# The last group of a Fourier turn gathered in two halves, and the last two dense blocks loaded after the last store

## The chip, the cores and the metric

The kernel runs on one core of one Trainium2 chip. The metric is the device time of one execution in microseconds (us). A profile of one execution is at hand: what each engine did and when, what it waited for, and what the DMA engines moved. TensorE (PE) multiplies matrices, VectorE (DVE) and ScalarE (ACT) work elementwise, GpSimd (POOL) too and more slowly; SyncE (SP) only issues DMAs, and ACT and GpSimd issue some as well. Each of these three has a DMA queue of its own: q1 is SP's, q10 is ACT's, q0 is GpSimd's.

## What is computed

```python
x = A_u                                             # 2048 positions x 512 channels
g = _sigmoid((x * gate_w).sum(-1, keepdims=True))   # one gate per position
a = _A_ref(x, ...)                                  # a long convolution (S4), by FFT, plus a skip term
b = _B_ref(B_x, ...)                                # dense 512 -> 1792, gelu, 1792 -> 512
return g * a + (1 - g) * b
...
K = jnp.einsum("dn,dnl,dn->dl", Cc, P, dB).real     # in _A_ref: a filter of 2048 taps per channel
Yf = Uf * Kf[None, :, :, :]                         # transforms of padded signal and filter, multiplied
y = irfft2(Yf, ...)[:, :, 0, :L]                    # back to positions
```

All of it is in float32; the dense products are made of three matmuls of split operands each (high and low parts).

## The kernel before

The kernel has two parts. `front` computes the dense layers, the filter taps and the first half of the transforms; a planner orders its instructions. `conv`, where the change lies, runs in the order in which it is written, and takes the last 120 us.

**What `conv` does.** A transform of 2048 positions is split into 32 outer by 64 inner steps. `conv` goes through 16 steps s, each with two of the 32 outer frequencies, n = 2s and 2s + 1. For each it transforms signal and taps (`signal`, `taps`, on TensorE), multiplies them (`product`, on VectorE) and transforms back over the inner index (`inverse`). The result of one n is a tile `pa` of 128 partitions by 512 channels. To sum over n, the data must be turned, so that n stands on partitions. `turn` does that through HBM: ScalarE copies `pa` to one of six buffers `sa`, a store of 256 KB writes it to the scratch `t4_d`, and when eight n (one group g of `GROUP` = 8) are stored, gathers bring rows of that group back into `t3`, whose partitions g, g + 4, g + 8, ... they fill. `seat` says on which partition of `t3` a frequency lies, and `constants` lays the rows of the matrix `g1` out to match.

**The queues.** Groups 0 to 2 are stored by SP and gathered by GpSimd, four gathers of 32 partitions by 8 rows of 512 (512 KB) each. Of group 3 the last store, n = 31, is on ACT's queue, and its gathers are eight of 256 KB, in turn on ACT's and SP's queues, since each of them has to wait for the stores to land. Between the stores, at steps 6 to 13, SP also loads eight "dense blocks" with `dense(k)`: the block k of the output that `front` has already written, (1 - g) b, for two tiles of 128 positions (512 KB).

**The end.** While the gathers are under way, TensorE makes late dense products (`rest`): for two position tiles, 2 and 3, seven products of the second dense layer each were put aside by `front`, one takes three matmuls. One of the fourteen runs before the last `inverse`, thirteen after it. A warm-up matmul (`N_KEEP` = 1, into `warm`) follows, and VectorE adds the two late sums to their dense block. Then comes the last turn, m = 0 to 7, called turn groups below: eight matmuls of 64 partitions by 32 columns, which sum over n and give two tiles of 128 positions (`pb`); each needs four of the 32 rows of `t3`. A tile is multiplied by its gate and added to the dense block, on VectorE in one operation, or, for the five tiles in `ASIDE`, by ScalarE and then GpSimd. SP stores each pair (512 KB) to the output, the pairs 0 and 7 tile by tile, the very last tile's on SP and the one before it by the list `(nc.sync, nc.scalar)`.

What sets the order here is the program text alone: each engine and each queue works through its own instructions in order, and waits where an operand is not there.

## Time and profile before

| | |
|---|---|
| median of 3 runs | 516.74 us (516.55 to 516.86) |
| profiled execution | 515.96 us |
| its span, first to last instruction | 514.2 us |
| TensorE busy | 497.0 us (97%) |
| VectorE, ScalarE, GpSimd busy | 427.7, 353.2, 38.7 us |
| DMA | 101.26 MB, 197 GB/s on average |
| granted clock of TensorE over the span | 0.992 |

Busy shares are averages over stages with different limits. TensorE's 97% says that the span is a chain of its work for most of the time, and nothing of the last 30 us, where the question is which transfer or engine comes last. Times below are counted from the span's start.

### The profile page before, as it was taken

To read this page: it belongs to the slowest core of one execution; us is meant where nothing else is said; L and a number is where in the kernel's file an instruction comes from. 1 tells how busy PE (TensorE), PEld (TensorE's weight loads), DVE (VectorE), ACT (ScalarE), POOL (GpSimd) and SP (SyncE) were. 2 spreads that over 40 slices of the span, in tenths; PEclk is the share of its full clock that TensorE was granted. 3 is DMA by queue.
4 is the path that set the end of the run, shared out by engine and by line. 5 is a ranking of instruction groups with operands and counts; after the bars stand their busy time and mean duration, and the time that the engine had idled before them with its cause. 6 is when DMAs were issued, how large, how long until landed. Compare 5 with 4: busy or idle time off the path is not lost.

```text
span 514.2 us, 11207 instructions
## 1 busy us (share of the span) xinstructions
PE 497.0 (97%) x4426; PEld 351.8 (68%) x4426; DVE 427.7 (83%) x794; ACT 353.2 (69%) x545; POOL 38.7 (8%) x74
## 2 busy tenths in 40 slices
PE   8998999989999999999999999999999999999992
PEld 5876787877777878788788888788787533333460
DVE  5989999989999999999999999999711675675533
ACT  6897959499995999977389958686354555555311
POOL 1000000000000000002300310002000001010113
PEclk9998999999999999999999999999999999999998
DMA  8989725172175727433950531716628999999977
GB/s 285 329 287 350 262 88 207 61 222 78 46 243 203 184 88 231 134 101 90 270 114 3 165 42 22 167 23 143 160 56 222 302 329 330 383 396 353 339 281 288
DMA packets 86805, 101.26 MB, mean 197 GB/s; under 512 B 38609, under 2 KB 58129, under 8 KB 86113
## 3 DMA queue, kind: packets, MB, share of 16 engines
q1 hardware_dynamic: 81216, 84.52, 49.8%
q0 software_dynamic: 5056, 14.45, 12.0%
q10 hardware_dynamic: 480, 1.57, 0.8%
q8 instruction: 35, 0.57, 0.5%
q14 instruction: 18, 0.14, 0.1%
HBM read 59.11 MB, written 41.42 MB: 196 GB/s over the span
## 4 chain that ended last, share of the span: by engine, by line
PE 64%; DVE 14%; issue 7%; ACT 7%; DMA 5%; SPq 1%; POOL 1%; POOLq 0%; DVEq 0%; ACTq 0%
PE pz L710 9%; PE ph L900 7%; PE ph L901 7%; PE ph L902 7%; PE acc L946 6%; PE acc L948 6%; PE acc L947 6%; PE p2k L1119 6%; PE p2u L1119 5%; PE pa L1158 5%; PE pz L426 2%; DVE y L675 2%; DVE y L688 2%; DVE loft L521 2%; DVE loft L520 1%
## 5 line engine op out<-in xcount | busy, mean ns | idle before, releaser
L900 PE MATMUL ph<-xh,wh 128*128 128x512 f32 x224 | 89.7, 400 | 1.7 <-ACT io L919 1.7
L901 PE MATMUL ph<-xlo,wh 128*128 128x512 f32 x224 | 88.2, 394 | 0.5 <-DVE xlo L827 0.4
L902 PE MATMUL ph<-xh,wl 128*128 128x512 f32 x224 | 88.0, 393 | 0.0
L946 PE MATMUL acc<-wh,hh 128*128 128x512 f32 x210 | 84.1, 400 | 0.7 <-ACT acc L952 0.7
L948 PE MATMUL acc<-wh,hl 128*128 128x512 f32 x210 | 82.1, 391 | 0.0
L947 PE MATMUL acc<-wl,hh 128*128 128x512 f32 x210 | 81.9, 390 | 0.0
L919 ACT ACTIVATE io<-ph,b1t 128x512 f32<-128x512 f32 x56 | 38.6, 690 | 34.8 <-PE ph L902 29.4
L710 PE MATMUL pz<-y,xc 128*32 128x64 f32 x2048 | 61.6, 290 | 0.4 <-DVE phase L620 0.4
L710 PEld LDWEIGHTS pz<-y,xc 128*32 128x32 f32 x2048 | 57.2, 136 | 6.7 <-issue 3.3
L928 DVE TENSOR_TENSOR hl<-io,hh 128x512 fp32r<-128x512 f32 x56 | 38.5, 687 | 22.7 <-ACT hh L920 22.5
L900 PEld LDWEIGHTS ph<-xh,wh 128*128 128x128 f32 x224 | 42.4, 189 | 14.3 <-ACT io L919 3.4
L901 PEld LDWEIGHTS ph<-xlo,wh 128*128 128x128 f32 x224 | 42.5, 190 | 10.4 <-DVE xlo L827 1.7
L946 PEld LDWEIGHTS acc<-wh,hh 128*128 128x128 f32 x210 | 39.4, 188 | 13.6 <-issue 3.8
L902 PEld LDWEIGHTS ph<-xh,wl 128*128 128x128 f32 x224 | 42.3, 189 | 9.2 <-DVE wl L827 0.3
L675 DVE TENSOR_TENSOR y<-y,ea 128x64 f32<-128x64 f32 (+4 forms) x80 | 45.3, 566 | 0.7 <-POOL y L665 0.4
L948 PEld LDWEIGHTS acc<-wh,hl 128*128 128x128 f32 x210 | 39.4, 188 | 9.0 <-DVE hl L928 0.5
L947 PEld LDWEIGHTS acc<-wl,hh 128*128 128x128 f32 x210 | 39.5, 188 | 7.7
L960 ACT ACTIVATE io<-acc,gate 128x512 f32<-128x512 f32 x30 | 20.3, 686 | 28.9 <-PE acc L948 28.9
L520 DVE TENSOR_TENSOR loft<-xc,zz 128x256 f32<-128x256 f32 (+2 forms) x48 | 37.3, 776 | 0.4
L521 DVE TENSOR_TENSOR loft<-xc,zz 128x256 f32<-128x256 f32 (+2 forms) x48 | 37.2, 774 | 0.0
L1141 DVE TENSOR_TENSOR v<-p2u,k 128x512 f32<-128x512 f32 x16 | 11.1, 691 | 31.1 <-ACT sa L1164 25.3
L688 DVE TENSOR_TENSOR y<-y,loft 128x2048 f32<-128x2048 f32 x16 | 36.6, 2285 | 0.2
(139 smaller groups left out, 840.1 us busy)
## 6 DMA issues: line engine op xcount, KB each, us to landing
tu_d<-attic SPq DMA_DIRECT2D x16, 512.0 KB, 3.5
tk_d<-sk SPq DMA_DIRECT2D x16, 512.0 KB, 6.8
tk<-tk_d SPq DMA_DIRECT2D x32, 256.0 KB, 5.9
t_d<-sa SPq DMA_DIRECT2D x31, 256.0 KB, 5.2
t<-t_d POOLq DMA_DIRECT2D x12, 512.0 KB, 6.9
attic<-tu_d SPq DMA_DIRECT2D x22, 256.0 KB, 4.7
attic<-in_xt_dram SPq DMA_DIRECT2D x20, 256.0 KB, 4.1
attic<-in_xs_dram SPq DMA_DIRECT2D x16, 256.0 KB, 5.3
```

What stands on the lines that cost most here:

```text
L520: vec(2 * m, lambda: vv.tensor_mul(t, a, br), due, [ka, *kb], [kt])
L521: vec(2 * m, lambda: vv.tensor_mul(v, a, bi), due, [ka, *kb], [kv])
L675: nc.vector.tensor_mul(both(n, 64 - 3 * n, n), both(0, 64 - n, n), an)
L688: v.tensor_mul(y[:, 0].rearrange("p (a b) c -> p a b c", a=2), e.rearrange("p (a b) c -> p a b c", a=2), cc,)
L710: nc.tensor.matmul(pk[32 * j : 32 * j + 32, gg // 4, gg % 4], x[:, r, :, ch], y[:, r, :, ch], start=(r == 0), stop=(r == 1), skip_group_ch ...
L900: nc.tensor.matmul(phs[q], h, xh[d], start=(d == 0), stop=False)
L901: nc.tensor.matmul(phs[q], h, xlo[d], start=False, stop=False)
L902: nc.tensor.matmul(phs[q], lo, xh[d], start=False, stop=(d == 3))
L946: nc.tensor.matmul(a, h, wh[1][f], start=(f == 0 and u >= NSB), stop=False, skip_group_check=True)
L947: nc.tensor.matmul(a, h, wl[1][f], start=False, stop=False, skip_group_check=True)
L948: nc.tensor.matmul(a, l, wh[1][f], start=False, stop=(f == FH - 1), skip_group_check=True)
L1119: nc.tensor.matmul(out[64 * i : 64 * i + 64], w, x, start=True, stop=True)
```

## The change

The last group is split by frequency: n = 24 to 27 and n = 28 to 31. The first half goes to a scratch `te_d` whose rows have 16 floats of padding, is gathered by GpSimd as soon as its four stores have landed, in four transfers of 8 partitions by 16 rows, and lies on partitions 3, 7, ..., 31 and 99, 103, ..., 127 of `t3` (the two ends). The second half goes to `tl_d` and lies on partitions 35, 39, ..., 95 (around the middle); all its stores are SP's, and its four gathers (16 partitions by 8 rows, 256 KB) are on ACT's and SP's queues. `seat` and `g1` follow. `dense(6)` and `dense(7)` leave steps 12 and 13 and stand behind the last store. Ten late products are made before the last turn instead of all, and the warm-up matmul is gone. The turn groups go 0, 2, 3, 4, 5, 6, 7, 1; the products left and the addition of the late sums come after the last of them, with the stores of pair 1, tile by tile. `ASIDE` names other tiles.

```diff
@@ constants
-N_KEEP = 1
+N_FIRST = 10
-ASIDE = (2, 4, 7, 9, 12)
+LATE = NT * (BLOCK[-1] + 1) - N_LATE
+ASIDE = (5, 6, 9, 11, 14)
@@ seat
-    return 4 * (n % 8) + n // 8
+    g, k = divmod(n, 8)
+    if g < 3:
+        return 64 * i + 32 * c + 4 * k + g
+    return 64 * i + 32 * (k // 4 ^ i) + 16 * c + 4 * (k % 4) + g
@@ scratch
-    t4_d = dr.tile([4, 2, 2, GROUP, 32, D], F32, name="t4_d")
+    t4_d = dr.tile([3, 2, 2, GROUP, 32, D], F32, name="t4_d")
+    te_d = dr.tile([2, 2, 4, 32, D + 16], F32, name="te_d")
+    tl_d = dr.tile([2, 2, 4, 32, D], F32, name="tl_d")
@@ turn
-                on = nc.sync if n < 31 else nc.scalar
-                on.dma_start(t4_d[g, :, :, k].rearrange("i c q d -> q (i c) d"), sa)
-                if k < GROUP - 1:
-                    continue
-                rows = t4_d[g].rearrange("i c k q d -> (i c k) q d")
-                w = 8 if n < 31 else 4
-                for h in range(0, 32, w):
-                    on = nc.gpsimd if n < 31 else (nc.scalar, nc.sync)[h // w % 2]
-                    on.dma_start(t3[g:P:4, h : h + w], rows[:, h : h + w])
+                to = t4_d[g, :, :, k] if g < 3 else (te_d, tl_d)[k // 4][:, :, k % 4, :, :D]
+                nc.sync.dma_start(to.rearrange("i c q d -> q (i c) d"), sa)
+                if g < 3 and k == GROUP - 1:
+                    rows = t4_d[g].rearrange("i c k q d -> (i c k) q d")
+                    for h in range(0, 32, 8):
+                        nc.gpsimd.dma_start(t3[g:P:4, h : h + 8], rows[:, h : h + 8])
+                if n == 27:
+                    for i in range(2):
+                        rows = te_d[i, :, :, :, :D].rearrange("c k q d -> (c k) q d")
+                        for h in range(0, 32, 16):
+                            nc.gpsimd.dma_start(t3[96 * i + 3 : 96 * i + 32 : 4, h : h + 16], rows[:, h : h + 16])
+                if n == 31:
+                    dense(6)
+                    dense(7)
+                    rows = tl_d.rearrange("i c k q d -> (i c k) q d")
+                    for h in range(0, 32, 8):
+                        on = (nc.scalar, nc.sync)[h // 8 % 2]
+                        on.dma_start(t3[35:96:4, h : h + 8], rows[:, h : h + 8])
@@ the end
-            if 6 <= s < 14:
+            if 6 <= s < 12:
                 dense(s - 6)
-        rest(14)
-        warm = ps.tile([P, D], F32, tag="pa", name="warm", bufs=2)
-        for _ in range(N_KEEP):
-            nc.tensor.matmul(warm[0:64], mats[7][0][1][:, 3], zs[0], start=True, stop=True)
-        for s in range(N_LATE):
-            n = NT - N_LATE + s
-            z = mos[n // 2][:, n % 2]
-            nc.vector.scalar_tensor_tensor(z, accs[n], gate[:, 1, n : n + 1], z, ALU.mult, ALU.add)
-        for m in range(8):
+        rest(N_FIRST)
+        order = [m for m in range(8) if m != LATE // 2] + [LATE // 2]
+        for k, m in enumerate(order):
...
+            if k == 7:
+                rest(14)
...
-                if m in (0, 7):
-                    (nc.sync, nc.scalar)[i if m else 0].dma_start(ov[m, :, i], z)
-            if 0 < m < 7:
+                if k == 0:
+                    nc.sync.dma_start(ov[m, :, i], z)
+            if 0 < k < 7:
                 nc.sync.dma_start(ov[m], mos[m])
+        for i in range(N_LATE):
+            z, g = mos[LATE // 2][:, i], gate[:, 1, LATE + i : LATE + i + 1]
+            nc.vector.scalar_tensor_tensor(z, accs[NT - N_LATE + i], g, z, ALU.mult, ALU.add)
+            (nc.sync, nc.scalar)[i].dma_start(ov[LATE // 2, :, i], z)
```

The names in the rows below: `sa0` to `sa5` are the buffers of the stores, `t4_d`, `te_d` and `tl_d` the scratches, `t3` the gathered data, `attic` and `loft` hold dense blocks, `out_0_dram` is the output; a number at a name's end is a buffer's running number, and `x4` is four in a row. SP's queue before, from the store of n = 22 to the first stores of the output:

```order
L1167 DMA t4_d_61<-sa0_4052 32x4x512
L1167 DMA t4_d_61<-sa1_4053 32x4x512
L1186 DMA attic_76<-out_0_dram 128x1024
L1167 DMA t4_d_61<-sa2_4054 32x4x512
L1167 DMA t4_d_61<-sa3_4055 32x4x512
L1186 DMA attic_76<-out_0_dram 128x1024
L1167 DMA t4_d_61<-sa4_4056 32x4x512
L1167 DMA t4_d_61<-sa5_4057 32x4x512
L1167 DMA t4_d_61<-sa0_4052 32x4x512
L1176 DMA t3_4066<-t4_d_61 32x2048 x4
L1260 DMA out_0_dram<-loft_77 128x512 x2
```

SP's queue in the changed kernel, from the store of n = 24 on:

```order
L1173 DMA te_d_62<-sa0_4054 32x4x512
L1173 DMA te_d_62<-sa1_4055 32x4x512
L1173 DMA te_d_62<-sa2_4056 32x4x512
L1173 DMA te_d_62<-sa3_4057 32x4x512
L1173 DMA tl_d_63<-sa4_4058 32x4x512
L1173 DMA tl_d_63<-sa5_4059 32x4x512
L1173 DMA tl_d_63<-sa0_4054 32x4x512
L1173 DMA tl_d_63<-sa1_4055 32x4x512
L1199 DMA attic_78<-out_0_dram 128x1024 x2
L1189 DMA t3_4068<-tl_d_63 16x4096 x2
L1268 DMA out_0_dram<-loft_79 128x512 x2
```

Two dense blocks that stood before the stores of n = 26 and n = 28 now stand between the last store, which has come over from ACT, and the gathers, of which SP has two instead of four.

TensorE before, from the last late product (three matmuls into `acc3`) to the first turn group (`pb00` and `pb01`):

```order
L1199 MATMUL acc3_4798<-wh15_125,hl5_153 128x512
L1197 MATMUL acc3_4798<-wh16_126,hh6_147 128x512
L1198 MATMUL acc3_4798<-wl16_140,hh6_147 128x512
L1199 MATMUL acc3_4798<-wh16_126,hl6_154 128x512
L1235 MATMUL warm_4820<-z0_4058,f17_4664 64x512
L1247 MATMUL pb00_4824<-t3_4066,g1t_4067 32x512
L1247 MATMUL pb01_4825<-t3_4066,g1t_4067 32x512
L1247 MATMUL pb00_4824<-t3_4066,g1t_4067 32x512
```

In the changed kernel, the same seam:

```order
L1210 MATMUL acc3_4800<-wh13_125,hh3_146 128x512
L1211 MATMUL acc3_4800<-wl13_139,hh3_146 128x512
L1212 MATMUL acc3_4800<-wh13_125,hl3_153 128x512
L1253 MATMUL pb00_4813<-t3_4068,g1t_4069 32x512
L1253 MATMUL pb01_4814<-t3_4068,g1t_4069 32x512
L1253 MATMUL pb00_4813<-t3_4068,g1t_4069 32x512
```

The seam lies three products earlier (`wh13` with `hh3`, not `wh16` with `hh6`), and the warm-up matmul is gone from it. And the end of TensorE's work in the changed kernel, from its last turn group (`pb10`, `pb11`) on:

```order
L1253 MATMUL pb10_4910<-t3_4068,g1t_4069 32x512
L1253 MATMUL pb11_4911<-t3_4068,g1t_4069 32x512
L1210 MATMUL acc3_4800<-wh14_126,hh4_147 128x512
L1211 MATMUL acc3_4800<-wl14_140,hh4_147 128x512
L1212 MATMUL acc3_4800<-wh14_126,hl4_154 128x512
L1210 MATMUL acc3_4800<-wh15_127,hh5_148 128x512
L1211 MATMUL acc3_4800<-wl15_141,hh5_148 128x512
L1212 MATMUL acc3_4800<-wh15_127,hl5_155 128x512
L1210 MATMUL acc3_4800<-wh16_128,hh6_149 128x512
L1211 MATMUL acc3_4800<-wl16_142,hh6_149 128x512
L1212 MATMUL acc3_4800<-wh16_128,hl6_156 128x512
```

The three products that left the seam stand here, behind the last turn group; before, a turn group came last.

## Rows read from the trace of the kernel before

**Rows 1.** Busy time by stage: PE, PEld, DVE, ACT, POOL; clock, DMA share, GB/s.

```profile
478.00:487.00 9.00, 9.00 (x37) 3.44 (x35) 5.16 (x9) 2.98 (x7) 0.62 (x2) 1.00 0.98 348
487.00:497.00 10.00, 10.00 (x42) 7.43 (x41) 1.50 (x2) 0.93 (x2) 0.00 (x0) 1.00 0.79 293
497.00:504.30 7.30, 7.30 (x129) 2.77 (x128) 5.77 (x9) 3.44 (x5) 4.35 (x4) 1.00 0.78 304
```

**Rows 2.** Timeline, the queues of SP and ACT: start, duration in us.

```profile
480.81 1.17 SPq L1167 DMA_DIRECT2D t_d<-sa  x2
...
484.64 3.34 SPq L1167 DMA_DIRECT2D t_d<-sa  x3
...
487.96 0.63 ACTq L1167 DMA_DIRECT2D t_d<-sa  x1
...
491.94 2.57 SPq L1176 DMA_DIRECT2D t<-t_d  x4
...
492.07 2.59 ACTq L1176 DMA_DIRECT2D t<-t_d  x4
...
501.25 1.58 SPq L1262 DMA_DIRECT2D out_dram<-loft  x2
...
506.81 1.12 SPq L1260 DMA_DIRECT2D out_dram<-attic  x1
```

**Rows 3.** DMA issues at 475.3, 480.8, 488.0, 491.9 (two), 506.8: us to landing last.

```profile
t_d<-sa SPq DMA_DIRECT2D x2, 256.0 KB, 2.7
...
t_d<-sa SPq DMA_DIRECT2D x2, 256.0 KB, 6.4
...
t_d<-sa ACTq DMA_DIRECT2D x1, 256.0 KB, 3.8
...
t<-t_d SPq DMA_DIRECT2D x1, 256.0 KB, 3.2
t<-t_d ACTq DMA_DIRECT2D x1, 256.0 KB, 3.7
...
out_dram<-attic SPq DMA_DIRECT2D x1, 256.0 KB, 6.3
```

**Rows 4.** Timeline, the engines from the last store on; brackets tell idle time before.

```profile
487.07 0.50 PE L1197 MATMUL acc<-wh,hh 128*128 128x512 f32 x1
...
495.82 0.39 PE L1199 MATMUL acc<-wh,hl 128*128 128x512 f32 x1
...
496.14 1.07 PE L1235 MATMUL warm<-z,f 128*64 128x512 f32 x2
...
497.14 7.17 PE L1247 MATMUL pb<-t,g1t 64*32 64x512 f32 x128
...
498.32 2.73 DVE L1258 SCALAR_TENSOR_TENSOR loft<-pb,gate,loft 128x512 f32<-128x512 f32 x4 [1.32 <-PE pb L1247]
...
499.95 2.52 POOL L1256 TENSOR_TENSOR loft<-loft,sa 128x512 f32<-128x512 f32 x2 [21.34 <-ACT sa L1255]
...
500.96 5.09 DVE L1258 SCALAR_TENSOR_TENSOR attic<-pb,gate,attic 128x512 f32<-128x512 f32 x7
```

**Rows 5.** DMA queues in 478:484 (two rows), 287:294, 502:511: packets, MB, share.

```profile
q0 software_dynamic: 150, 1.74, 82.8%
q1 hardware_dynamic: 144, 0.53, 22.6%
...
q0 software_dynamic: 979, 1.79, 92.8%
...
DMA  6999999998989999999999999999999999999999
...
DMA packets 1076, 3.55 MB, mean 395 GB/s; under 512 B 110, under 2 KB 110, under 8 KB 1075
```

**Rows 6.** TensorE's timeline at 40.7, and the stretch 41.5:44.9 by engine.

```profile
40.71 1.34 PE L426 MATMUL pz<-attic,c1t 32*64 32x256 f32 x32 [2.07 <-ACT attic L457]
...
41.50:44.90 3.40, 3.40 (x23) 2.35 (x8) 3.40 (x10) 3.40 (x5) 0.00 (x0) 0.50 1.04 383
```

More of the change, by code (lines that the diff above doesn't have):

```diff
@@ L101, in k0_order, with seat @@
     return [8 * (n % 4) + n // 4 for n in range(32)]
-def seat(n):
-    return 4 * (n % 8) + n // 8
+def seat(n, i, c):
+    g, k = divmod(n, 8)
+    if g < 3:
+        return 64 * i + 32 * c + 4 * k + g
+    return 64 * i + 32 * (k // 4 ^ i) + 16 * c + 4 * (k % 4) + g
 def constants():
@@ L124, in constants @@
     c1 = np.concatenate([np.stack([er, ei], 2).reshape(32, 64)] * 4, 0)
-    rows = np.zeros((2, 64, 32))
+    g1 = np.zeros((P, 32))
     for n, k in enumerate(k0_order()):
-        rows[:, seat(n)] = er.T[k] / L
-        rows[:, seat(n) + 32] = ei.T[k] / L
-    g1 = rows.reshape(P, 32)
+        for i in range(2):
+            g1[seat(n, i, 0)] = er.T[k] / L
+            g1[seat(n, i, 1)] = ei.T[k] / L
     ko = k0_order()
@@ L1165, in turn @@
                 g, k = divmod(n, GROUP)
-                on = nc.sync if n < 31 else nc.scalar
-                on.dma_start(t4_d[g, :, :, k].rearrange("i c q d -> q (i c) d"), sa)
-                if k < GROUP - 1:
-                    continue
-                rows = t4_d[g].rearrange("i c k q d -> (i c k) q d")
-                w = 8 if n < 31 else 4
-                for h in range(0, 32, w):
-                    on = nc.gpsimd if n < 31 else (nc.scalar, nc.sync)[h // w % 2]
-                    on.dma_start(t3[g:P:4, h : h + w], rows[:, h : h + w])
+                to = t4_d[g, :, :, k] if g < 3 else (te_d, tl_d)[k // 4][:, :, k % 4, :, :D]
[5 more added lines that the diff above has]
+                if n == 27:
+                    for i in range(2):
+                        rows = te_d[i, :, :, :, :D].rearrange("c k q d -> (c k) q d")
[8 more added lines that the diff above has]
+                        on.dma_start(t3[35:96:4, h : h + 8], rows[:, h : h + 8])
         accs, mos = {}, {}
@@ L1228, in conv @@
             turn(s)
[L1229 removed]
+            if 6 <= s < 12:
                 dense(s - 6)
[L1231 to L1242 removed]
+        rest(N_FIRST)
+        order = [m for m in range(8) if m != LATE // 2] + [LATE // 2]
+        for k, m in enumerate(order):
+            tag, n = ("pa", 2) if k % 3 == 2 else ("pu", 4)
             pbs = [ps.tile([P, D], F32, tag=tag, name=f"pb{m}{i}", bufs=n) for i in range(2)]
```

1 line of the change is left out of this document (removed).

## The prediction, made before the changed kernel had run

> **What bounds the kernel now.** I read the end first, because the diff touches only the last 40 us. By stage, TensorE is busy nearly all of 478 to 504, but what it does from 487 on is filling: thirteen late dense products from 487.07 to 496.2 and a warm-up matmul to 497.2 [rows 1, 4]. What it waits for stands in the queues. The last store of the turn, n = 31, is issued on ACT's queue at 487.96 and lands 3.8 us later, at 491.7 [rows 2, 3]. Only then may the eight gathers of the last group go, four on SP (491.94) and four on ACT (492.07), 2.1 MB in all; their first two land after 3.2 and 3.7 us, at 495.2 and 495.8 [rows 2, 3]. The DMA share of that stage is the lowest of the three (0.78 and 0.79 against 0.98) [rows 1]. The last turn ("turn groups" below: eight groups of eight matmuls, 0.9 us each) starts at 497.14 and takes 7.17 us [rows 4]. So at its start the data was there 1.3 us earlier, and TensorE's filling came last.
>
> After it the order is: VectorE from 498.32 to 506.05 nearly without a gap, GpSimd 1.26 us for each tile put aside, and the stores [rows 4]. The second turn group's store leaves SP at 501.25 [rows 2]; from 502 to 511 the DMA engines move 3.55 MB at 395 GB/s without a slack slice [rows 5]. The last store is issued at 506.81 and lands 6.3 us later, at 513.1 [rows 2, 3]. A store that is queued for 6.3 us instead of 2.7 has some 3.6 us of others ahead of it. So the end is: start of the second turn group (497.14 + 0.9 = 498.0), 3.2 us to its store, then 3.7 MB at the DMA's rate, then a fixed close. A microsecond off the second group's start is a microsecond off the end; one off VectorE's last operation is nothing while that backlog lasts.
>
> **The change, part by part.** *Half of the last group goes early.* Frequencies 24 to 27 get a scratch of their own (te_d); once those four stores have landed, GpSimd gathers them (1.05 MB). What stays behind store 31 is four gathers, 1.05 MB instead of 2.1. *The last two dense blocks* (1.05 MB) leave their places among the stores and go between store 31 and SP's gathers. Bytes up to store 31 are equal: minus 1.05, plus 1.05.
>
> When does store 31 land? It is now SP's, right behind store 30, whose issue ends at 484.64 + 3.34 = 487.98 [rows 2]; so 488.0, as before. Its time to land is bounded by two rows: 2.7 us for stores that met a short queue, 6.4 us for stores 26 and 27, issued into GpSimd's third gather [rows 3]. The rest of the queue is gone by then: stores 26 and 27 had a dense block of 0.52 MB ahead of them, 1.4 us at the 377 GB/s of that stretch (1.74 + 0.53 MB in 6 us) [rows 5], so they land near 486.4, stores 28 and 29 soon after. But the early gather, issued at 486.5 and moving from about 488 (estimate: its four issues and a start of about 1 us), runs just beside stores 30 and 31. I take 3.5 us, between the bounds and nearer to the lower one because its rows are 2 KB pieces like the stores' and not 16 KB: landing at 491.5.
>
> The rate between two queues shows in the third gather: GpSimd's queue with 16 KB rows moved 1.74 MB while SP's, with work waiting, moved 0.53 [rows 5]. [...]
>
> *The first turn group* then needs ACT's first gather: issued 0.33 us after the landing as before, landed 3.7 us later: 491.5 + 0.3 + 3.7 = 495.5. Three of the four early gathers must be there too: at the 257 GB/s that GpSimd's queue made alone with 2 KB rows [rows 5], 1.05 MB takes 4.1 us from 488, so 492.1, and 493 with the landing; cover 2 us.
>
> *TensorE's filling.* Ten products instead of thirteen before the turn: each is 0.68 us (thirteen in 487.07 to 496.2), so TensorE is free at 493.9, 1.6 us before the data. The warm-up matmul (1.07 us) goes. Both cost nothing and stop being the last thing.
>
> *The second turn group* needs SP's first gather, which stands behind the dense blocks on SP's queue. Alone these take 2.7 us at 395 GB/s from about 490.8, to 493.5; SP's gathers would begin to move near 492.9, so 0.6 us are lost there. By bytes it is tighter: from 488 the early gather, stores 30 and 31, the dense blocks and the first two gathers are 3.1 MB, 8.0 us at 390 GB/s, so 496.1 and about 0.6 us to land: 496.7. That is 0.3 us after the time at which TensorE could take it (495.5 + 0.9). I take 496.7 for the second group, against 498.0: **minus 1.3 us**. Bounds: store 31 after 2.7 us gives 495.9, minus 2.1; after 6.4 us it gives 499.4 or later, plus 1.4.
>
> *The two late tiles go last.* Tile pair 1 is turned at the end, the three products left (2.1 us) follow, and VectorE adds two operations of 0.74 us behind its eleven. VectorE's end moves from 8.9 us after the first group's start (506.05) to 10.4, so 505.9, and TensorE's last product to 495.5 + 0.9 + 0.3 + 7.2 - 0.9 + 2.3 = 505.3, ahead of it. The stores ahead keep the DMA busy until the last two (0.52 MB, 1.3 us) would begin, about 513.1 - 1.3 - 1.3 - 1.0 = 509.5: cover about 3 us, and it would be paid one for one beyond it. The tiles put aside keep their count (five) and nearly their places among the groups; zero. GpSimd has nothing between its four new issues and its first addition, 499.95 in the profile [rows 4].
>
> Sum on the profiled execution: 515.96 - 1.3 = 514.7. The runs' median is 516.74, 0.8 above the profiled one; the difference is put on it: **515.4**.
>
> **The rivals.** (1) *The early gather holds up the last stores*, as the third one did: landing at 488.0 + 5.2 to 6.4, 493.2 to 494.4. Second group 498.2 to 499.4, so 516.9 to 518.1. For it: SP's stores landed late each time GpSimd gathered. Against: 16 KB rows then, 2 KB rows now. 0.16. (2) *The change doesn't do what it says:* the dense blocks fill no hole but push SP's gathers back, a full microsecond beyond my 0.3; the early half is won and given back: 516.4. 0.13. (3) *TensorE's clock.* Without the filler, TensorE is idle for 1.6 us at 493.9, and longer if store 31 is late. [...] 0.07. (4) *Slower: the early gather runs on half the engines.* Its transfers have 8 partitions each, where the ones in the trace have 32. If each uses eight engines, and all four the same eight, it has half of 257 GB/s: three of four take 6.1 us from 488; those engines also carry half of the stores and dense blocks (0.79 MB at 198 GB/s, 4.0 us). It lands near 499, and the first group starts there instead of the second at 498.0: about plus 1.9, 518.6. It decides if the third early gather lands after 497.1. [...] 0.10.
>
> **How the numbers follow.** Forecast 0.54, at 515.4 with its own range 514.3 to 516.2. 0.2% is 1.0 us, about what a measurement of this kernel can tell from no change. Faster: 0.48 of the forecast and 0.05 of rival 2, 0.53. Same: 0.06, 0.08 of rival 2, 0.12 of rival 1, 0.06 of rival 3, 0.02 of rival 4: 0.34. Slower: 0.04, 0.01 and 0.08: 0.13. The range goes from 513.9 (store 31 after 2.7 us, less the runs' scatter of 0.3) to 517.5, which leaves out most of rival 4 and the worst of rival 1.
>
> **What would show it.** Right: store 31 landed by 492, the first turn group at 495 to 496 waiting for a DMA and not for TensorE, the second within 1.2 us of it, VectorE's last operation 4 us or more before the last landing. Wrong: landing of stores 30 and 31 after 493 (rival 1); a gap of over 1.5 us between the first two groups with SP's gather as releaser (2); a granted clock of 0.5 between 495 and 503 (3); a first group that waits for GpSimd's gather (4); or VectorE's end within 3 us of the last landing, the cover that I counted on.

## The result, and the profile after

| | before | changed kernel |
|---|---|---|
| median | 516.80 us (516.55 to 516.86) | 521.34 us (521.02 to 524.98) |
| ratio | | 1.0104, 95% interval 1.0065 to 1.0142 |
| profiled execution | 515.96 us | 524.98 us |

The changed kernel is 4.5 us slower, where 1.3 us less was forecast; 521.3 lies above the forecast's range of 513.9 to 517.5. Its profiled execution is the longest of the four; the same kernel, run once more for a second trace, took 521.64 us. That second trace (e1_again) is read first, since it is near the median; "the first trace" is that of the 525.0 us.

The second trace's timeline from the last two stores on (start and duration in us; the brackets tell idle time and what ended it) answers to [rows 2] and [rows 4]:

```profile
487.23 2.54 POOL L1182 DMA_DIRECT2D t<-te_d  x4 [8.23 <-DMA te_d<-sa]
...
487.71 1.16 SPq L1173 DMA_DIRECT2D tl_d<-sa  x2
...
488.96 1.57 SPq L1199 DMA_DIRECT2D attic<-out_dram  x2
...
493.81 1.39 SPq L1189 DMA_DIRECT2D t<-tl_d  x2
...
493.89 1.36 ACTq L1189 DMA_DIRECT2D t<-tl_d  x2
...
500.72 9.27 PE L1253 MATMUL pb<-t,g1t 64*32 64x512 f32 x128 [6.32 <-DMA t<-tl_d]
```

The first turn group starts at 500.72, after 6.32 us in which TensorE waited for a late gather; before it started at 497.14 and waited for nothing but TensorE's own filling. Store 31 is issued 0.6 us behind store 30's 487.71, so at 488.32. The DMA issues of that stretch, one row per issue, answer to [rows 3] (last number: us to landing). They are store 31 (488.32), the first dense block (488.96), SP's first late gather (493.81) and ACT's (493.89):

```profile
tl_d<-sa SPq DMA_DIRECT2D x1, 256.0 KB, 5.4
...
attic<-out_dram SPq DMA_DIRECT2D x1, 512.0 KB, 8.3
...
t<-tl_d SPq DMA_DIRECT2D x1, 256.0 KB, 6.6
t<-tl_d ACTq DMA_DIRECT2D x1, 256.0 KB, 6.7
```

Store 31 took 5.4 us to land and not 3.8, and a late gather 6.7 us and not 3.7. So the turn waits on the path that was to become shorter: 12.4 us from store 31's issue (5.4 + 0.2 + 6.7 + 0.1) to the first turn group, against 9.2 before. By stage (columns as in [rows 1]; the last row is the stretch of the low clock, read by itself):

```profile
478.00:487.00 9.00, 9.00 (x39) 3.44 (x35) 5.40 (x9) 3.08 (x6) 0.99 (x2) 1.00 0.92 336
487.00:494.40 7.40, 7.40 (x32) 5.55 (x30) 0.00 (x0) 1.07 (x2) 2.48 (x4) 1.00 0.84 243
494.40:500.70 6.30, 0.00 (x1) 0.01 (x1) 0.00 (x0) 0.00 (x0) 0.00 (x0) 0.81 0.92 326
500.70:510.00 9.30, 9.28 (x129) 2.92 (x129) 6.04 (x9) 3.44 (x5) 4.66 (x4) 0.76 0.43 167
...
498.40:505.10 6.70, 4.38 (x48) 1.41 (x56) 2.04 (x3) 0.53 (x1) 0.00 (x0) 0.50 0.36 140
```

Two things stand there. TensorE is idle for all of 494.4 to 500.7, and its granted clock falls in that stage and is still low in the next, at 0.50 from 498.4 to 505.1: the turn groups take 9.27 us instead of 7.17 [rows 4]. The second turn group starts at 502.40, 4.4 us later than before (498.02). And the DMA engines are busy for 0.84 of 487 to 494.4 but move only 243 GB/s, less than the 293 GB/s at a share of 0.79 in [rows 1]: they are not idle, they are slow.

In the first trace the loss is larger, and it lies elsewhere. Store 31, issued at 489.07, landed as soon as forecast, and the late gathers, issued at 491.65 (SP) and 491.74 (ACT), were late by more:

```profile
tl_d<-sa SPq DMA_DIRECT2D x1, 256.0 KB, 2.5
...
t<-tl_d SPq DMA_DIRECT2D x1, 256.0 KB, 10.2
t<-tl_d ACTq DMA_DIRECT2D x1, 256.0 KB, 8.9
```

The turn even started and stopped again, for one of GpSimd's early gathers:

```profile
500.79 1.88 PE L1253 MATMUL pb<-t,g1t 64*32 64x512 f32 x2 [5.62 <-DMA t<-tl_d]
...
504.08 9.04 PE L1253 MATMUL pb<-t,g1t 64*32 64x512 f32 x126 [1.41 <-DMA t<-te_d]
```

From the first turn group to the last landing of the output it is 16.0 us before (497.14 to 513.14) and 17.9 us in the second trace (500.72 to 518.57). Counted from store 31's issue, the last landing comes 5.1 us later than before; 3.2 of them lie ahead of the first turn group and 1.9 behind it.

### The profile page after: what moved, and what is told of

Read it like the earlier page. It is cut to its first block, busy times and chain, and to the rows that moved or that the text cites. A ratio compares the mean times of both kernels' runs of the same rounds, so it can differ in the third digit from the quotient of the medians.

```text
span 523.2 us, 11199 instructions
## 1 busy us (share of the span) xinstructions
PE 499.9 (96%) x4424; PEld 352.0 (67%) x4424; DVE 427.6 (82%) x794; ACT 353.1 (67%) x545; POOL 41.3 (8%) x78
## 4 chain that ended last, share of the span: by engine, by line
PE 61%; DVE 20%; DMA 8%; ACT 6%; issue 2%; SPq 1%; POOL 0%; DVEq 0%; POOLq 0%; ACTq 0%
PE pz L716 8%; PE ph L906 6%; PE ph L907 6%; PE ph L908 6%; PE acc L952 6%; PE p2u L1125 6%; PE p2k L1125 5%; PE acc L954 5%; PE acc L953 5%; PE pa L1164 5%; DMA t<-te_d 3%; DVE loft L527 2%; DVE y L694 2%; PE pz L432 2%; DVE y L681 2%; DVE loft L526 2%
## 5 line engine op out<-in xcount | busy, mean ns | idle before, releaser
L1147 DVE TENSOR_TENSOR v<-p2u,k 128x512 f32<-128x512 f32 x16 | 11.1, 691 | 31.2 <-ACT sa L1170 25.3
```

## The experiments

Executions differ in when store 31 is issued (487.8 to 490.0 in all but one of the traces), which lies ahead of the part in question. So the table counts from that issue: to the start of the first turn group, and to the last landing of the output, both read from each run's own trace. Times are medians, ratios are against the kernel before on the same chip. A trace is of one execution, and not always of one near the median: that of e10 took 526.4 us, that of e16 516.3. Edits are shown against the changed kernel, with parts left out, unless the text names another.

| run | time, us | ratio, 95% interval | to the turn | to the end |
|---|---|---|---|---|
| before | 516.2 to 517.0 | 1 | 9.2 | 25.2 |
| e1_again: changed kernel | 521.64 | 1.0104, 1.0065 to 1.0142 | 12.4 | 30.2 |
| e2_dense_back | 520.00 | 1.0061, 1.0038 to 1.0083 | 10.4 | 27.9 |
| e3_early_on_act | 522.80 | 1.0123, 1.0098 to 1.0149 | 14.7 | 31.1 |
| e4_end_only | 515.85 | 0.9994, 0.9974 to 1.0013 | 8.4 | 24.6 |
| e5_no_pad | 523.35 | 1.0143, 1.0122 to 1.0164 | 13.7 | 31.6 |
| e6_warm | 520.65 | 1.0090, 1.0074 to 1.0105 | 11.8 | 28.0 |
| e7_early_free | 525.19 | 1.0187, 1.0131 to 1.0243 | 7.8 | 24.2 |
| e8_end_warm | 516.63 | 1.0005, 0.9990 to 1.0021 | 8.0 | 24.2 |
| e9_spread | 522.73 | 1.0113, 1.0084 to 1.0141 | 12.8 | 29.3 |
| e10_spread_no_pad | 524.17 | 1.0146, 1.0104 to 1.0189 | 16.1 | 34.1 |
| e11_behind | 521.82 | 1.0105, 1.0072 to 1.0138 | 12.4 | 30.5 |
| e12_behind_dense_last | 519.15 | 1.0059, 1.0039 to 1.0080 | 9.7 | 26.7 |
| e13_behind_ends | 519.90 | 1.0058, 1.0040 to 1.0075 | 11.4 | 28.4 |
| e14_behind_middle | 521.65 | 1.0077, 1.0051 to 1.0103 | 9.8 | 31.4 |
| e15_swap | 521.71 | 1.0098, 1.0060 to 1.0136 | 13.2 | 29.2 |
| e16_dense_behind | 514.78 | 0.9971, 0.9957 to 0.9985 | 7.2 | 23.2 |
| e17_dense_last | 516.51 | 0.9999, 0.9987 to 1.0011 | 6.6 | 24.9 |
| e18_dense_old_end | 516.72 | 1.0001, 0.9992 to 1.0011 | 9.2 | 25.3 |

The ratio beside e1_again is that of the changed kernel's first comparison. In e13 the landing of SP's last store is missing from the trace, in e15 that of ACT's, so 28.4 and 29.2 are lower bounds. In e14 the turn stopped again after two matmuls, until 13.2 us. In the first trace of the changed kernel the turn started after 11.7 us, stopped until 15.0, and the end came at 32.8.

### What the changed kernel's parts do, one at a time

**The same kernel again.**

> The changed kernel once more, unchanged, for a second trace: the first was of an execution of 525.0 us, while the three others took 521.0 to 521.5. If the late landing of the early gather (504.0 in the first trace) and the half clock of the turn groups make the loss, both are here too, only smaller: last early gather at 500 to 502, time 521.0 to 521.6. Rival: in the usual executions the early gather is in time and the 4.5 us come from the end (stores, VectorE); then the second turn group starts by 498 here.

521.64 us, and both things are there, but the early half was back sooner than expected: it landed in 4.7 to 9.2 us, its last piece at 498.4; the clock fell. The turn waited for a late gather, not for the early half. The rival (the loss is in the end) fell at once, as the second turn group started at 502.4.

**The dense blocks back in steps 12 and 13.**

```diff
-                    dense(6)
-                    dense(7)
-            if 6 <= s < 12:
+            if 6 <= s < 14:
```

> The changed kernel with the two dense blocks back in steps 12 and 13; nothing is left out. Theory A (three transfers of 1.05 MB each share the engines from 491 on, 3.15 MB in 12 us in the first trace): one of the three is gone, so the gathers end about 4 us earlier, 517 to 518. Theory B (the early gather is slow in itself, since each of its transfers has 8 partitions and at most 9 of its packets were under way at a time until 500.5): 520 to 521.

520.0 us, at the lower end of theory B's range. Its trace has a clean view of the early gather, since nothing else moved beside it for 3 us. The queues in 493 to 496 (packets, MB, share of the 16 engines; a packet that reaches over the edge counts whole):

```profile
DMA packets 338, 0.73 MB, mean 243 GB/s; under 512 B 160, under 2 KB 160, under 8 KB 338
...
q0 software_dynamic: 338, 0.73, 102.7%
```

All sixteen engines were busy with GpSimd's early gather, and made 243 GB/s. So it was not half of the engines, as rival 4 of the prediction had it; but the early gather is slow even alone.

**The early gather on ScalarE's queue.**

```diff
-                if n == 27:
+                if n == 31:
...
-                            nc.gpsimd.dma_start(t3[96 * i + 3 : 96 * i + 32 : 4, h : h + 16], rows[:, h : h + 16])
+                            nc.scalar.dma_start(t3[96 * i + 3 : 96 * i + 32 : 4, h : h + 16], rows[:, h : h + 16])
```

> The changed kernel with the four early transfers issued by ScalarE, behind its last copy and ahead of its late gathers, instead of GpSimd; nothing is left out. Theory A: the same bytes at the same time, 520.5 to 522. Theory C (GpSimd's queue is what is slow: 0.6 us per issue and 1.4 us from the first issue to the first packet): ScalarE's queue starts sooner, and the early half lands 1 to 3 us earlier, 518 to 520; its late gathers come up to 2 us later.

522.80 us, above the ranges of both theories: taking the early half off GpSimd's queue did not make it faster. On ScalarE's queue its packets moved from 490.0 to 501.9. ScalarE's late gathers stand behind the early ones there: the first landed 14.5 us after store 31's issue (488.50 to 503.0), in e1's trace 12.3.

**The new end alone, on the kernel before.**

```diff
-        rest(14)
+        rest(N_FIRST)
...
-        for m in range(8):
+        order = [m for m in range(8) if m != LATE // 2] + [LATE // 2]
+        for k, m in enumerate(order):
...
```

> The kernel before with the changed end alone (ten products before the turn, no warm-up matmul, pair 1 last, the other list of tiles put aside); the gathers, stores and dense blocks are the old ones. If the loss is all in the gathers: 516.0 to 517.2, the same as the kernel before. Rival: the end itself costs, as VectorE's two additions, GpSimd's list and the last products come after everything: 517.5 to 519.

No measurable difference (0.9974 to 1.0013). In its trace the turn starts 0.8 us earlier after store 31, and the end comes 0.5 us earlier. Its ten times fall in two groups, six at 514.9 to 515.9 us and four at 517.9 to 518.3; no run here tells what parts them.

**The padding.**

```diff
-    te_d = dr.tile([2, 2, 4, 32, D + 16], F32, name="te_d")
+    te_d = dr.tile([2, 2, 4, 32, D], F32, name="te_d")
```

> The changed kernel with the early scratch's rows left unpadded; nothing is left out. Theory A (the early gather is slow by the form of its pieces: its packets of 4 KB took about 300 ns each while it had the engines for itself, where a dense block's took 159): with 16 rows in one piece of a partition its packets are 16 KB and take about 610 ns, as GpSimd's other gathers did, so 1.05 MB costs the engines 2.5 us and not 4.7: first turn group 2 us earlier, 518.5 to 519.7. Theory B (its 8 partitions keep it to half the engines): now the pieces are larger and the split can only be worse, 521 to 524. Rival C: the larger pieces starve the last stores, as group 2's gather did, 521 to 523.

523.35 us: theory A fell. The time lies in theory B's range, and rival C's starved stores were there: store 31 took 9.5 us to land. From 488.3 to 496 the trace has never more than eight of GpSimd's data packets under way at a time, where e2 has 14 to 18 in 493 to 496; so without the padding the early gather did use about half of the engines.

**The clock.**

```diff
         rest(N_FIRST)
+        warm = ps.tile([P, D], F32, tag="pa", name="warm", bufs=2)
+        for _ in range(6):
+            nc.tensor.matmul(warm[0:64], mats[7][0][1][:, 3], zs[0], start=True, stop=True)
```

> The changed kernel with six warm-up matmuls of 1.04 us each behind the ten products, so that TensorE is busy from 494.4 to about 500.7, when the first turn group's data came in the second trace. If the half clock after the idle time (0.5 from 498.35 to 505.18) costs what the turn groups lengthened by (9.27 against 7.17 us), the time falls by 1.5 to 2.1 us, to 519.3 to 520. Rival: the output's stores hide it, and the time stays at 521 to 521.6.

The granted clock stayed up (1.00 over the turn groups), and they ran in 7.16 us again:

```profile
495.64 5.36 PE L1247 MATMUL warm<-z,f 128*64 128x512 f32 x12
...
501.35 7.16 PE L1256 MATMUL pb<-t,g1t 64*32 64x512 f32 x128 [0.34 <-DMA t<-tl_d]
```

From the first turn group to the last landing it is 16.2 us, close to the 16.0 before, against 17.9 in e1's trace: the idle TensorE cost 1.6 us behind it. The median went from 521.34 to 520.65, less than expected and inside the two intervals; the traces show the price, the medians don't settle it.

**No early gather.**

```diff
-                if n == 27:
+                if n == 15:
...
-                            nc.gpsimd.dma_start(t3[96 * i + 3 : 96 * i + 32 : 4, h : h + 16], rows[:, h : h + 16])
+                                nc.gpsimd.dma_start(t3[p : p + 13 : 4, h : h + 16], t4_d[1, i, c, 0:4, h : h + 16])
```

> The changed kernel with the early gather taken away: the partitions of frequencies 24 to 27 are filled with rows of group 1 at n = 15 instead, so that half of the last group is left out of the sum. It prices the early gather. If its share of the DMA engines and of the queues between 488 and 498 is what makes the change slow, stores 30 and 31 land at 491.5 or earlier, the first turn group starts at 495 to 496, and the time is 514 to 516. Rival: the dense blocks behind the last store do it; then the late gathers still land behind 499, and it is 518 to 520.

The run leaves half of the last group out of the sum. Its time answers nothing: the eight small gathers that stand in the early one's place (4 partitions each) took 9.5 to 13.6 us, beside group 1's, and SP's stores issued meanwhile landed after up to 20.0 us, so that the whole tail came some 9.6 us late. But its tail is then undisturbed, and tells what was asked. Store 31 (497.95), ACT's first late gather (500.66) and the turn:

```profile
tl_d<-sa SPq DMA_DIRECT2D x1, 256.0 KB, 2.5
...
t<-tl_d ACTq DMA_DIRECT2D x1, 256.0 KB, 5.0
...
505.77 7.26 PE L1254 MATMUL pb<-t,g1t 64*32 64x512 f32 x128 [1.69 <-DMA t<-tl_d]
```

Without the early gather it is 7.8 us from store 31 to the turn, about what was forecast (7.5), with the dense blocks where the change puts them. The early gather makes it 12.4 in e1's trace: 2.9 us on the store, 1.7 on the late gather. In the first trace it makes it 11.7 to the start and 15.0 to where the turn goes on, with nothing on the store.

**The new end with the clock kept** (the edit against e4).

```diff
         rest(N_FIRST)
+        warm = ps.tile([P, D], F32, tag="pa", name="warm", bufs=2)
+        for _ in range(2):
+            nc.tensor.matmul(warm[0:64], mats[7][0][1][:, 3], zs[0], start=True, stop=True)
```

> The kernel before with the changed end alone, as in the run of that, plus two warm-up matmuls behind the ten products: TensorE is busy from 494.6 to 496.7 and the first turn group's data was there at 496.8. Nothing is left out. If the idle 2.2 us there lower the clock and cost time (the last seven turn groups took 7.88 us), 514.5 to 515.5; if not, 515.9 as without.

The same time as the kernel before (0.9990 to 1.0021), and no gain over e4; the idle 2.2 us in e4 cost nothing that shows in the time, though the granted clock over e4's turn groups was 0.81.

### Why the early gather is slow

The early half lies on partitions 3 to 31 and 99 to 127, eight in each transfer. The next runs vary where it lies.

**Both halves on partitions 8 apart.**

```diff
-    return 64 * i + 32 * (k // 4 ^ i) + 16 * c + 4 * (k % 4) + g
+    return 64 * i + 32 * c + 8 * (k % 4) + 4 * (k // 4) + g
...
+                        nc.gpsimd.dma_start(t3[3:P:8, h : h + 8], rows[:, h : h + 8])
...
-                        on.dma_start(t3[35:96:4, h : h + 8], rows[:, h : h + 8])
+                        on.dma_start(t3[7:P:8, h : h + 8], rows[:, h : h + 8])
```

> The changed kernel with the two halves of the last group on partitions 8 apart over the whole tile, so that each early transfer has 16 partitions by 8 rows and not 8 by 16; the padding stays, and nothing is left out. Theory B (few partitions make the early gather slow: without padding its 16 KB packets took 1.2 to 2.1 us on at most 8 engines, where the late gathers' with 16 partitions took 0.61): its 4 KB packets take about 160 to 200 ns instead of 210 to 300, it is over 2 us earlier, and the time is 518.5 to 520. Rival (the padded pieces are what is slow): 521 to 522.

> The same with the padding gone too: 16 partitions and 16 KB packets. Theory B: the early gather runs as GpSimd's other gathers do, 1.05 MB in 2.7 us; but such packets hold up stores 30 and 31, as group 2's gather did stores 26 and 27, to about 5 us after their issue, so that the first turn group starts at 498 to 499: 518 to 519.5. Rival: the stores are starved for the whole of it, as without padding on 8 partitions (9.5 us): 520 to 522.

Both expectations were missed, the rivals' ranges too: 522.73 and 524.17 us. Sixteen partitions in a transfer didn't help, and now the late gathers were slow as well, from the same scratch, by the same queues, with the same pieces. The queues while only late gathers ran, in 498 to 500, first of e1_again (partitions 35 to 95, 4 apart), then of e9 (8 apart):

```profile
DMA packets 94, 0.78 MB, mean 389 GB/s; under 512 B 46, under 2 KB 46, under 8 KB 46
...
q10 hardware_dynamic: 48, 0.46, 54.1%
q1 hardware_dynamic: 45, 0.31, 38.5%
```

```profile
DMA packets 51, 0.42 MB, mean 209 GB/s; under 512 B 25, under 2 KB 25, under 8 KB 25
...
q1 hardware_dynamic: 25, 0.26, 64.9%
q10 hardware_dynamic: 25, 0.15, 36.1%
```

The engines are as busy (the two shares make 93% and 101%) and move half as much. What differs is the set of partitions that is written. The count of partitions in a transfer is the same, and so are the rows of each.

**The early half behind the last store, on SP's queue.** Here the partitions are 8 apart and unpadded, and the dense blocks stand in steps 12 and 13 (e11) or behind SP's late gathers (e12).

```diff
                 if n == 31:
+                    early = te_d.rearrange("i c k q d -> (i c k) q d")
+                    for h in range(0, 32, 8):
+                        nc.sync.dma_start(t3[3:P:8, h : h + 8], early[:, h : h + 8])
```

> The halves on partitions 8 apart, no padding, and the early gather on SP's queue behind the last store instead of on GpSimd's, so that it runs in the 2.4 us in which that store lands; the dense blocks are back in steps 12 and 13. Nothing is left out. If the idea of the change holds once the early half no longer competes with stores 30 and 31: store 31 lands at 491.7 to 492.5, the late gathers (1.05 MB) land by 496 to 497, and the time is 515 to 516.5. Rival: the early half takes the late gathers' place on the engines, which start only when it is through: 517 to 518.5.

> As the one before, with the two dense blocks behind SP's late gathers instead of in steps 12 and 13. Stores 28 to 31 meet a shorter queue: store 31 lands at 490.7 to 491.5, the late gathers at 495 to 496, and the time is 514.5 to 516. Rival: the dense blocks share the engines with the late gathers and the first stores of the output, and what was won is given back: 516 to 517.5.

Store 31 landed 2.4 us after its issue in e12 (4.5 in e11, where the dense blocks stand ahead of the last stores), so its contest with the early half was gone, and e12 is, with e13 below, the best of the kernels with an early half (519.15 us, ratio 1.0059). But both are 3 us and more over what was expected: early and late half ran one after the other, and the early half, alone, moved at 225 GB/s, where e1's late gathers made 389. SP's queue in e12, 491.5 to 495, early half alone:

```profile
DMA packets 96, 0.79 MB, mean 225 GB/s; under 512 B 48, under 2 KB 48, under 8 KB 48
...
q1 hardware_dynamic: 96, 0.79, 107.2%
```

**The change's own partitions, and the halves exchanged.** e13 and e14 keep the early half behind the last store, at the two ends and in the middle; e15 changes of the change only which half lies where, and with it the form of the transfers: a half in the middle goes in four of 16 partitions by 8 rows, one at the ends in four of 8 by 16.

```diff
-    return 64 * i + 32 * (k // 4 ^ i) + 16 * c + 4 * (k % 4) + g
+    return 64 * i + 32 * (1 - k // 4 ^ i) + 16 * c + 4 * (k % 4) + g
...
+                    for h in range(0, 32, 8):
+                        nc.gpsimd.dma_start(t3[35:96:4, h : h + 8], rows[:, h : h + 8])
```

> The change's own partitions, no padding; the early gather stands on SP's queue behind the last store, the two ends in turn, and the dense blocks behind SP's late gathers. Nothing is left out. Theory P (the rate hangs on the partitions that are written at the same time): the late gathers, in the middle, run at 0.61 us a packet; the early ones, 8 partitions a transfer, at 1.2 to 2.1 us as on GpSimd's queue, unless both ends run at once: first turn group at 496.5 to 498, 516.5 to 518.5. Rival Q (GpSimd's queue was the trouble): the early half runs at 0.61 us too, first turn group at 495.5, 514.5 to 516.

> As the one before with the halves exchanged: the early half in the middle (16 partitions, 8 rows), the late half at the two ends, 8 partitions by 16 rows, one end on each queue. Theory P: the early packets take 0.61 us (1.05 MB in 2.7 us), the late ones 1.2 us or more, so the last data comes 2 to 3 us later than with the halves as they were; 517 to 519.5. Rival Q: the same time as the one before, within 0.7 us.

> The changed kernel with the halves exchanged and nothing else: GpSimd gathers the early half, padded, into the middle, in four transfers of 16 partitions by 8 rows; the late half goes to the ends. Theory P: the early packets of 4 KB take about 160 ns and not 210 to 300, stores 30 and 31 land a microsecond sooner, but the late half is slow now: 520 to 523. Rival R (padded pieces are slow on GpSimd's queue whatever the partitions): the early packets still take 210 to 300 ns, and the time is 521 to 524.

e15 has the comparison in the changed kernel itself. The same half, padded as in the change, by the same queue, beside the same stores and dense blocks, but into the middle. First e1_again in 489 to 497 (early half to the ends), then e15 in 490 to 495.7 (to the middle):

```profile
DMA packets 965, 2.34 MB, mean 292 GB/s; under 512 B 273, under 2 KB 273, under 8 KB 964
...
q1 hardware_dynamic: 506, 1.37, 52.1%
q0 software_dynamic: 459, 0.96, 46.4%
```

```profile
DMA packets 676, 2.22 MB, mean 390 GB/s; under 512 B 88, under 2 KB 88, under 8 KB 674
...
q1 hardware_dynamic: 390, 1.27, 55.9%
q0 software_dynamic: 286, 0.95, 42.4%
```

GpSimd's 0.96 MB took 46.4% of 8 us, which is 259 GB/s with all engines; its 0.95 MB in e15 took 42.4% of 5.7 us, 393 GB/s. The neighbours gain too: SP's queue goes from 329 to 399 GB/s by the same sum. So rival R (padded pieces are slow anywhere) fell. That it is not the form either, 8 partitions by 16 rows, shows in e9: there GpSimd's early gather had e15's form, 16 by 8 and padded, on partitions 8 apart, and in 489 to 494 it made 291 GB/s by the same sum:

```profile
q0 software_dynamic: 272, 0.90, 61.9%
```

Store 31 gained less than theory P said (5.1 us to land, 5.4 in e1), and the time didn't improve (521.71 us), since now the late half goes to the ends. It is slow there for another reason. Its gathers ran at 254 GB/s in 497 to 500, but with the engines busy for 0.60 of the time, on ACT's and SP's queues:

```profile
q10 hardware_dynamic: 22, 0.49, 38.1%
q1 hardware_dynamic: 22, 0.26, 21.4%
```

By the sum above that is about 430 and 405 GB/s with all engines: the engines that worked were not slowed, the others had nothing to do. The packet records say the same: from 497.5 to 500.4 eight of these transfers' data packets were under way at a time (nine at most), of both queues together, where e9's late gathers had 15 to 17. So transfers of 8 partitions on these two queues used about half of the engines, which is the mechanism of the prediction's rival 4, in a place that it did not name.

e13 and e14 fit both: with the early half at the ends, or the late one, some part is slow wherever it stands in the queue. In e13 the early half at the ends, on SP's queue, had eight data packets under way for 97% of 491.2 to 495. Why these packets, of 32 KB, took 1.55 us each (median) and those of e15's late half, also of 32 KB, 1.21 us, is open. Their times, 519.90 and 521.65 us, are 1.4 and 2.2 us over the upper ends for theory P, so it has the direction and not the size. The intervals of their ratios overlap, so the times don't decide against rival Q; e9's slow late gathers, which were on SP's and ACT's queues, and e12's early ones on SP's do. No kernel here has both halves on partitions that are written at 389 to 393 GB/s, as e1's late half and e15's early half are, so how much of the 4.5 us the choice of partitions costs by itself is not shown.

By the partitions that are written, with the engines busy (93, 103 and 101% by the shares above): 35, 39, ..., 95 made 389 GB/s (e1's late gathers), the eight at either end 243 (e2's early), and partitions 8 apart over the whole tile 209 (e9's late). By what mechanism the partitions set the rate is not shown.

### The dense blocks alone

Left over is the part of the change that the early gather had covered: the two dense blocks behind the last store. e16 is e4 with the blocks between the last store and SP's gathers, e17 has them behind SP's gathers, and e18 is e16's move with the old end. The edit of e16 against e4:

```diff
+                if n == 31:
+                    dense(6)
+                    dense(7)
                 w = 8 if n < 31 else 4
...
-            if 6 <= s < 14:
+            if 6 <= s < 12:
```

> The kernel before with the changed end and the two dense blocks between the last store and SP's gathers; no split, no early gather; nothing is left out. If the dense blocks fill the hole behind the last store, store 31 lands at 490.5 to 491.3 (2.4 us after its issue, as in the runs with the early half behind the stores), the first gathers at 494.5 to 495.8, and the time is 515 to 516, 0.1 to 0.4% under the kernel before. Rival: SP's four gathers are pushed back, the second turn group waits for them, 516.5 to 518.

> The same with the dense blocks behind SP's gathers. The gathers come first: first turn group at 494.5 to 495.5, second right behind it, and VectorE's last groups wait for the dense blocks until 502 to 503 if at all: 514.5 to 515.8. Rival: the dense blocks land at 504 or later and hold up turn groups 6 and 7, whose stores then end the kernel: 516.5 to 518.

> The kernel before with one edit: the two dense blocks between the last store and SP's gathers. Nothing is left out. If the hole in the transfers alone makes the gain, 514.5 to 515.5. If the new end is needed (with thirteen products and the warm-up matmul TensorE is busy until 9 us after the last store's issue, and the first turn group can't start sooner), 516 to 517.

e16 is faster than the kernel before, 514.78 against 516.68 us, ratio 0.9971 (0.9957 to 0.9985). Its traced execution is one of its longer ones (516.29 us), with store 31 issued at 489.80, 1.8 us later than before; it took 3.1 us to land, not the expected 2.4. The hole behind the last store is used (3.0 to 5.2 us behind store 31's issue: 491 to 493.2 in the kernel before, then 492.84 to 495.04 in e16):

```profile
DMA packets 6, 0.01 MB, mean 3 GB/s; under 512 B 3, under 2 KB 3, under 8 KB 6
```

```profile
DMA packets 236, 0.90 MB, mean 410 GB/s; under 512 B 29, under 2 KB 29, under 8 KB 223
```

e17 starts the turn soonest of all and gains nothing: its hole stays (72 GB/s in 490.5 to 493), and the dense blocks then share the engines with the first stores of the output. From 493 to 512 it moves 7.15 MB at 377 GB/s with next to no slack; so the end looks like a sum of bytes there: the turn starts 2.6 us earlier than before, the last store lands 0.3 us earlier. e18 fills the hole and gains nothing either, because thirteen products and the warm-up matmul hold the turn at 9.2 us after store 31 (first row e17, then two of e18):

```profile
494.76 3.14 PE L1245 MATMUL pb<-t,g1t 64*32 64x512 f32 x48 [0.35 <-DMA t<-t_d]
```

```profile
496.82 1.07 PE L1238 MATMUL warm<-z,f 128*64 128x512 f32 x2
...
497.82 7.17 PE L1250 MATMUL pb<-t,g1t 64*32 64x512 f32 x128
```

So neither the new end (0.9994) nor the move of the dense blocks (1.0001) shows a gain alone, and together they are worth 1.5 us (0.29% by the ratio). That the move needs the new end is clear of the noise (e18's interval and e16's don't meet), and e18's trace shows why. That the new end needs the move is likely and not shown: e4's interval, 0.9974 to 1.0013, overlaps with e16's.

## Why the prediction was wrong, step by step

- **What bounds the kernel** was read rightly as far as the runs show it. That the turn waited for TensorE's filling is shown by e4 and e18, that the hole behind the last store was free by e16. That the end moves with the start of the turn holds in e16 (both 1.9 us earlier) and about in e4 (0.8 and 0.5), and not in e17, where the dense blocks' bytes come behind it. The minus 1.3 us of the forecast is about what e16 made (minus 1.5), by the dense blocks and the new end. That the two numbers are alike is luck: the forecast's gain was to come with the early half, the change's main part, and that has no share in e16's.
- **The bytes: the step that failed.** The second turn group was put at 496.7 by the sum "3.1 MB, 8.0 us at 390 GB/s"; it started at 502.4 in e1's trace. The sum used 257 GB/s for when the early half lands [rows 5] and counted its bytes at 390 when asking what is left for the others. The early gather at 254 to 259 GB/s with all engines (the two traces) took the engines' time for about 1.5 times its bytes, against 393 in e15. With its own 257 in the sum it comes to 9.4 us and 498.0 (an estimate: 4.1 us for the early half, 5.3 for the other 2.05 MB, 0.6 to land), as late as before. And the neighbours were slowed too: e1's trace moved 2.34 MB in 489 to 497, 292 GB/s in all, and the first trace, with the engines busy for 0.99 of 491 to 501, no more:

```profile
DMA packets 840, 2.83 MB, mean 283 GB/s; under 512 B 332, under 2 KB 332, under 8 KB 777
...
q0 software_dynamic: 414, 0.75, 29.5%
```

  The early gather's 0.75 MB in 29.5% of 10 us are 254 GB/s with all engines, as in e1. That, and the dense blocks ahead of it, make the late gather's 6.7 us against the forecast's 3.7 (5.0 without the early gather, e7). The cause, partitions that are written at 209 to 259 GB/s where others get 389 to 393, was in no term and in no rival. The 257 itself came out right (243 to 259 GB/s here) by luck: the row that it was read from is of 2 KB packets, the early gather's data packets are of 4 KB, and the same pieces made 393 GB/s into the middle (e15).
- **Store 31** was forecast to land after 3.5 us, between 2.7 and 6.4. In e1's trace, where GpSimd issued its first early gather 1.1 us ahead of it, it took 5.4; in the first trace, where that gather came 0.5 us behind it, 2.5, and 2.4 to 2.5 in runs without that contest (e7, e12, e13). So rival 1, held at 0.16, came in one trace and not in the other, and the loss is there in both. Store 31 and ACT's first late gather together take 12.1 us in e1's trace and 11.4 in the first, where 7.2 were forecast: the early half's time on the engines is paid by the one or by the other. The lean to the lower bound rested on pieces of 2 KB, like the stores'; the early gather's data packets came as 4 KB. No run shows the 3.5 us, an estimate, or the size of the pieces by itself: beside the same 4 KB packets the store took 5.4 us and 2.5, and 9.5 beside e5's 16 KB ones, which also used about half of the engines.
- **The early gather's arrival** was given a cover of 2 us: forecast to be there at 493. Its third piece landed at 496.8 and its last at 498.4 in e1's trace (504.0 and 504.3 in the first). It was ahead of the late half in one and last in the other, so the cover was gone.
- **Rival 4** had the right part under suspicion, for a reason that did not hold in the changed kernel: e2 shows all sixteen engines busy with the padded transfers of 8 partitions. On about half of the engines, by the eight or nine packets under way at most, such transfers ran in e5 (without padding), and on SP's and ACT's queues in e13 and e15. Its price of plus 1.9 us is less than half of the 4.5: it left SP's and ACT's late gathers at their old time, and the clock out. Its sign, the third early gather landing after 497.1, was there in the first trace (504.0), where the turn did wait for GpSimd's gather, and not in e1's (496.8), where the late gathers decided.
- **The clock, rival 3**, was held at 0.07, with an idle time forecast at 1.6 us, shorter than the one before the low clock of [rows 6]. It became 6.3 us, the granted clock fell to 0.50, and turn groups that took 7.2 us took 9.3: 1.6 us at the end by e6's trace, about what the 3.4 us at half clock of that row would cost (1.7, an estimate). It does not stand beside the others as a case of its own; it follows from any of them that makes TensorE wait, and belonged in their prices.
- **Rival 2**, SP's gathers pushed back by the dense blocks, did not decide: SP's first late gather landed 0.2 us before ACT's in e1's trace (6.6 us from 493.81, 6.7 from 493.89), and 1.2 us behind it in the first, where the turn waited for the early half longer still. The dense blocks do have a price, larger than the 0.6 us that the forecast gave them: ACT's first late gather, which the forecast left at 3.7 us, took 5.0 in e7.
- **The end** (late tiles last, VectorE's cover) was priced at zero and shows none (e4, e8).

Chances and range went wrong together: rivals 1, 3 and 4 were given as alternatives, each alone, and the range cut off the two dearest. They hang together by the early gather's time on the engines and the wait that it makes, and they add up: 5.1 us between the traces of before and e1.

## What to carry to other kernels

Here a gather at a reduced rate slowed what ran beside it too (SP's queue 329 GB/s beside the early gather's 259 in e1, 399 beside 393 in e15), so price such a transfer by the engine time that it takes, not by its bytes. Before a tile is split into parts that are gathered apart, ask which partitions each part writes, and how many each transfer has; at e9's 209 GB/s the half, 1.05 MB, would take 5.0 us, and the whole at e1's 389 5.4 (estimates). And when two edits each show no gain, try them together before dropping either: here a shorter filling and a filled hole were worth 1.5 us as a pair.

## What the hardware showed that I had not expected

- Gathers into 16 partitions 4 apart (35 to 95) made 389 GB/s, the same rows into 16 partitions 8 apart 209 GB/s, with the engines busy all the time in both (e1, e9).
- Transfers of 8 partitions at the ends of the tile: padded, on GpSimd's queue, they kept 14 to 18 data packets under way and made 243 GB/s (e2); on ACT's and SP's queues, unpadded, eight packets under way and 254 GB/s, with the engines busy for 0.60 of the time (e15).
- Gathers into 4 partitions each, by GpSimd, took 9.5 to 13.6 us for 128 KB beside other gathers, and stores queued on SP meanwhile took up to 20.0 us to land (e7).
- The late gathers' packets came long after their issue while slow transfers held the engines: 6.6 to 6.8 us to land for each queue's first in e1 and e2, 3.1 to 3.8 in e16 and e17. How the engines choose between queues was not settled.
